# Respacing loads, in-place output blocks and weight differences in a fused attention and expert kernel

One core of one Trainium2 chip runs the kernel. The metric is the device time of one execution in microseconds, as the median of several. A run is called slow below when it is over 1.5% above the fastest of the same kernel; with one core there is no second die to compare with, so slow is only a matter of the time.

## The reference, cut

```python
def _attn_ref(x, state):            # x 8x8x512x64, state 8x8x32x64
    a = softmax(x @ state^T / 8);   xread = a @ state
    a2 = softmax(state @ x^T / 8);  sread = a2 @ x
    return concatenate([xread, sread], axis=2)      # 544 rows per batch and head

def _moe_ref(x, w_in, w_out, s, b): # x 4352x512, w_in 512x2048, w_out 2048x512
    r = maximum(x @ w_in, 0)
    return (s * (r * r) + b) @ w_out
```

The softmax lines are shortened; the reference subtracts the maximum and adds 1e-9 to the sum. All is given and returned in fp32.

## The kernel before

The kernel works on the eight batches as eight stages of 21 us. In a stage TensorE multiplies the hidden layer of one batch (`h`), the output of the batch before it (`oA`, `oB`, `oC`) and the scores of the next (`T`). The output product saves one multiplication in eight: it uses sums and differences of squares (`s`, formed by `token_sum`) and of weights (`wd`, formed by `weight_sums`), and drains banks A, B and C of PSUM (the memory that TensorE writes its sums into) several times. The parts that the change touches, with cuts marked by `# ...`:

```python
# the end of a block of the hidden layer: relu, then a square on VectorE or ScalarE
if key == 1 and f in (5, 9):
    with tc.issue_after(nc.cur_bb.bb.instructions[-1]):
        nc.scalar.square(gt[:, f % 4 - 1 : f % 4 + 1], r16)
elif f % 2 == 1:
    nc.vector.tensor_mul(gt[:, f % 4 - 1 : f % 4 + 1], r16, r16)
    G["last"] = nc.cur_bb.bb.instructions[-1]

# an output block: drain a bank of PSUM into a staging buffer (3 of them), then store it
def put(bank, add, j, n0):
    # ...
    osb = opool.tile([P, ni, NH], FP32, name=f"osb_{b}_{j}_{n0}", tag="osb")
    # ...
    nc.vector.scalar_tensor_tensor(osb, acc[bank], s_bc, add, ALU.mult, ALU.add)
    # ...
    nc.gpsimd.dma_start(dst[j][:, :, n0 : n0 + NH], osb)
# "add" is the bias for A, and the kept blocks u3, qb, u2 (one buffer each) for C, B, C
```

```python
# the opening
nc.scalar.dma_start(ident16, ident_dr.ap())
# ... two loads of half of batch 0's x, 512 KB each, on SyncE's queue
nc.scalar.dma_start(stf[:, 0:2, :], st_v[:, 0:2, :])
# ...
warm_up(11)                         # matmuls without use, 128x512
# ... casts of x
att_xT_pe(0, 0)                     # x transposed on TensorE, with ident16
att_stT(0)                          # state transposed on TensorE, with ident16
# ...
warm_up(2)
att_T(0, [0])                       # first scores

# stage s: f counts 16 steps of the hidden layer; at(f, ...) puts work behind step f
if s == 1:
    at(8, lambda: att_xT_dma(3))    # x of batch 3 transposed by DMA, SyncE's queue
    at(12, lambda: load_x(4))       # x of batch 4, 512 KB, GpSimd's queue
    # ...
if s == 2:
    at(1, lambda: load_x(5))
elif s in (3, 4):
    at(1, lambda: load_x(s + 3))
# ...
at(4, lambda: att_ET(nb))           # exponentials of the next batch transposed by DMA
at(8, lambda: att_shares(nb))       # VectorE: den (sums of ET), shares
if s in (2, 3):
    at(6, lambda: att_xT_dma(nb + 1))
at(9, lambda: att_a4_dma(nb))       # shares transposed by DMA
if s == 2:
    at(9, stT_dma)
elif s in (3, 4):
    at(9, lambda: att_xT_dma(s + 3))
```

The softmax here doesn't subtract the row's maximum and nothing guards it: scores larger than these inputs give would overflow.

Of the kernel before, what the change touches and what calls it, by code (L numbers as in the profile page):

```python
# [14 lines left out]
def kernel(  # L15
# [10 lines left out]
    nc = tc.nc  # L26
# [69 lines left out]
    stf = konst.tile([P, 2 * NPE, D], FP32, name="stf")  # L96
# [21 lines left out]
    def load_x(b):  # L118
        new_xn(b)
        nc.gpsimd.dma_start(  # L120
            out=xn[b].rearrange("p h c d -> p h (c d)"),
            in_=x[b].rearrange("h (q c) d -> q h (c d)", q=P),
        )
# [18 lines left out]
    A = {b: {} for b in range(B)}  # L142
# [59 lines left out]
    def att_xT_dma(b):  # L202
        xT = new_xT(b)
        nc.sync.dma_start_transpose(
            out=xT.rearrange("p h k t -> p (h k) t"),
            in_=xn[b].rearrange("p h c d -> p (h c d)"),
        )
# [180 lines left out]
    def mm1_close(key, hps, ntok, f):  # L388
        if f % 2 == 0:
            R2[key] = rpool.tile([P, 2, ntok], FP16, name=f"r_{key}_{f}", tag="r")  # L390
        r16 = R2[key]
        if key == 0 and f in (1, 5):
            nc.vector.tensor_scalar(r16[:, f % 2], hps, 0.0, None, ALU.max)
        else:
            nc.scalar.activation(r16[:, f % 2], hps, AF.Relu)  # L395
            G["relu"] = nc.cur_bb.bb.instructions[-1]
        if f % 4 == 0:
            G4[key, f // 4] = gpool.tile([P, 4, ntok], FP16, name=f"g_{key}_{f}", tag="g")
        gt = G4[key, f // 4]
        G[key, f] = gt[:, f % 4]  # L400
        if key == 1 and f in (5, 9):
            with tc.issue_after(nc.cur_bb.bb.instructions[-1]):
                nc.scalar.square(gt[:, f % 4 - 1 : f % 4 + 1], r16)
        elif f % 2 == 1:
            nc.vector.tensor_mul(gt[:, f % 4 - 1 : f % 4 + 1], r16, r16)  # L405
            G["last"] = nc.cur_bb.bb.instructions[-1]
# [111 lines left out]
    def fast_items(b):  # L518
# [41 lines left out]
        def put(bank, add, j, n0):  # L560
            if b == "sr":
                ends.append(own[1][:, len(ends) : len(ends) + 1])
                osb = ends[-1]
            else:
                osb = opool.tile([P, ni, NH], FP32, name=f"osb_{b}_{j}_{n0}", tag="osb")
            if bank == "C" and b == last_b:
                for i in range(ni):
                    nc.vector.scalar_tensor_tensor(
                        osb[:, i], acc["C", i], s_bc, add[:, i], ALU.mult, ALU.add
                    )  # L570
            else:
                nc.vector.scalar_tensor_tensor(osb, acc[bank], s_bc, add, ALU.mult, ALU.add)  # L572
            if b == "sr":
                for i in range(4):
                    dst = out_BSn[4 * j + i, S:ST, n0 : n0 + NH]
                    eng = nc.sync if i % 2 else nc.scalar
                    eng.dma_start(dst, osb[Ns * i : Ns * i + Ns, 0])
                return
            if b == "0b":
                nc.gpsimd.dma_start(x_dst(0, 2 + j)[:, n0 : n0 + NH], osb[:, 0])  # L580
                return
            dst = out_BSn[b, 0:S].rearrange("(q ci cj) n -> cj q ci n", ci=2, cj=2)
            nc.gpsimd.dma_start(dst[j][:, :, n0 : n0 + NH], osb)  # L583
# [74 lines left out]
    def bias_sum():  # L658
        ps = att_ps([P, DM], FP32, "wsum_ps")
        wsum = apool.tile([P, 2, DM], FP16, name="wsum", tag="W", bufs=1)  # L660
        for i in range(NKF // 4):
            for q in range(4):
                mm(
                    ps[32 * q : 32 * q + 32, :],
                    ones16,
                    wof(4 * i + q),
                    start=(i == 0),
                    stop=(i == NKF // 4 - 1),
                    tp=(0, 32 * q),
                )  # L670
        nc.vector.tensor_copy(wsum[:, 0], ps)
        nc.vector.tensor_sub(wsum[:, 1], ps, wsum[:, 0])
        A["wsum"] = wsum

    def bias_end():
# [18 lines left out]
    def warm_up(n):  # L694
        wps = psO.tile([P, 512], FP32, tag="o", name="warm_ps")
        for _ in range(n):
            mm(wps, warm[:, 0:P], warm)
# [12 lines left out]

    with tc.manual_schedule(engines={ET.PE, ET.SP, ET.Pool}):
        nc.vector.memset(warm, 0.0)
        nc.scalar.dma_start(ident16, ident_dr.ap())
        for g in range(NG):
            nc.sync.dma_start(
                xf[:, g],
                x[0, g :: NG].rearrange("h (q c) d -> q h (c d)", q=P),
            )
        nc.scalar.dma_start(stf[:, 0:2, :], st_v[:, 0:2, :])
        nc.scalar.preload_act_table_set("natural_log_exp_and_others")  # L720
        nc.sync.dma_start(stf[:, 2:4, :], st_v[:, 2:4, :])
        nc.sync.dma_start(sb_row[:, 0:1], moe_s.to_broadcast((1, 1)))
# [31 lines left out]
        nc.gpsimd.dma_start(out=st16[:, 4:, 0, :], in_=st_v[:, 4:, :])  # L754
        load_x(2)

        warm_up(11)
        cast_x0(0, 0, nc.vector.tensor_copy)
        cast_x0(0, 1, nc.scalar.copy)
        att_xT_pe(0, 0)  # L760
        att_stT(0)
        cast_x0(1, 0, nc.vector.tensor_copy)
        warm_up(2)
        att_T(0, [0])
# [37 lines left out]
        def pieces(s):  # L802
            nb = s + 1
            out = {}

            def at(f, fn):
                out.setdefault(f, []).append(fn)

            def ahead(f, fn):
                out.setdefault((f, "ahead"), []).append(fn)  # L810

            if s == 1:
                at(0, lambda: att_xT_dma(2))
                at(0, gated_x3)
                at(0, lambda: att_ET(0))
                at(0, lambda: att_ET(1))
                at(8, lambda: att_xT_dma(3))
                at(12, lambda: load_x(4))
                at(2, lambda: att_M(1, 2, "act"))
                ahead(3, bias_sum)  # L820
                at(4, bias_end)
                at(3, lambda: att_M(1, 3, "act"))
                at(6, lambda: att_stT(2))
                at(10, bias_half)
                at(8, lambda: att_M(2, 0, "act"))
                at(8, lambda: att_M(2, 1, "act"))
                at(10, lambda: att_M(2, 2, "act"))
                at(10, lambda: att_T(2, [0, 1]))
                at(11, lambda: att_ET(2))
                at(12, lambda: att_D(2, [0, 1]))  # L830
                at(13, lambda: att_M(2, 3, "act"))
                at(13, lambda: att_V(0))
                return out
            if s == 2:
                at(1, lambda: load_x(5))
            elif s in (3, 4):
                at(1, lambda: load_x(s + 3))
            if nb < B:
                if nb < NST:
                    at(0, lambda: att_stT(nb))  # L840
                ahead(4, lambda: att_M(nb, 0, "later"))
                ahead(4, lambda: att_T(nb, [0, 1]))
                ahead(4, lambda: att_M(nb, 1, "later"))
                at(4, lambda: att_ET(nb))
                at(4, lambda: A[nb]["M", 0]())
                at(6, lambda: A[nb]["M", 1]())
                at(8, lambda: att_shares(nb))
                if s in (2, 3):
                    at(6, lambda: att_xT_dma(nb + 1))
                at(9, lambda: att_a4_dma(nb))  # L850
                if s == 2:
                    at(9, stT_dma)
                elif s in (3, 4):
                    at(9, lambda: att_xT_dma(s + 3))
            if s == 2:
                at(1, lambda: att_srT_dma(0))
                at(8, lambda: att_V(1))
                at(12, lambda: att_srT_dma(1))
            ahead(4 if s == last_b else 10, lambda: att_V(s))
            if nb < B:  # L860
                ahead(10, lambda: att_M(nb, 2, "later"))
                ahead(10, lambda: att_M(nb, 3, "later"))
                at(10, lambda: A[nb]["M", 2]())
                at(12, lambda: A[nb]["M", 3]())
            if s == last_b:
                at(6, lambda: att_srT(s))
            else:
                at(12, lambda: att_srT_dma(s))
            if s == last_b:
                for i in range(4):  # L870
                    at(12 + i, lambda i=i: mm1_sr(i))
            return out
# [4 lines left out]
        for s in range(1, B):  # L877
# [16 lines left out]
            for f in range(NKF):  # L894
# [23 lines left out]
                    fn()  # L918
                if s == 1:
                    with tc.issue_after(G["last"]):  # L920
                        for _ in range({0: 2, 1: 1, 2: 1, 6: 1, 7: 1, 8: 1, 9: 1}.get(f, 0)):
                            sums.pop(0)()
                        for i, j in {0: [(1, 0), (2, 0)], 1: [(1, 1), (2, 1)], 7: [(3, 0)], 8: [(3, 1)],
                                     10: [(4, 0), (4, 1)]}.get(f, []):
                            token_sum("0b", i, j)
                for fn in items[f]:
# [57 lines left out]
```

## Time and profile before

| | before |
|---|---|
| time, median of 3 (range) | 209.41 us (209.28 to 209.71) |
| span of the profiled run | 208.0 us |
| TensorE busy | 198.5 us (95%) |
| end of its last matmul | 203.73 us |

The waits and lines at the four gaps of TensorE that the change aims at stand in the prediction below. Five more lines, of the timeline of before, are needed for what came. The columns are the start in us, the duration in us, engine (a "q" means a DMA being issued), line, operation, output and inputs; in brackets stands the idle time in front of it with what ended it.

```profile
7.36 0.59 PE L70 MATMUL warm_ps<-warm 128*128 128x512 f16 x2
...
96.05 1.01 POOL L120 DMA_DIRECT2D xn<-in_x_dram  x1
...
103.59 2.17 SPq L330 DMA_TRANSPOSE ET<-E  x1
...
109.22 1.22 DVE L278 TENSOR_REDUCE den<-ET 128x32 f32<-128x1024 f16 x1
...
111.83 0.60 PE L70 MATMUL oC<-wo,s 128*128 128x256 f16 x4
```

The load of batch 7's x leaves 7.5 us ahead of the transpose ET. ET is issued at 103.59, landed at 108.60 by its semaphore (5.0 us), `den` reads it without a wait, and behind `den` VectorE drains bank C in time for the oC at 111.83, which waits for nothing. In the first line two warm-up matmuls take 0.59 us together and start 0.22 us apart; the eleven at the start came every 0.43 us. So TensorE's array, the grid that multiplies, ran at half its rate at first and at full rate by 7.36.

### The profile page before, as it was taken

How to read it: one execution, taken by the hardware profiler on the slowest of the kernel's cores; microseconds unless marked ns; L12 is line 12 of the kernel's file. 1: busy time of each engine (PE TensorE's matmuls, PEld its weight loads, DVE VectorE, ACT ScalarE, POOL GpSimd, SP SyncE). 2: the span in 40 equal slices, each digit the busy share in tenths (PEclk: the TensorE clock that was granted, in tenths of full speed). 3: DMA queues.
4: the chain of work that ended last, by engine and by line, in shares of the span. 5: the costliest groups of instructions: out<-in, count | busy, mean ns of one | idle time of the engine just before them, and what ended most of it. 6: DMA issues, size and time to landing. Idle time of an engine off the chain costs nothing.

```text
span 208.0 us, 4853 instructions
## 1 busy us (share of the span) xinstructions
PE 198.5 (95%) x1971; PEld 133.0 (64%) x1971; DVE 163.4 (79%) x286; ACT 128.5 (62%) x254; POOL 39.3 (19%) x66
## 2 busy tenths in 40 slices
PE   7988999998999999999999999999999999999991
PEld 2433333555766676667676667676767777788881
DVE  1479688987859996799779966997699786796861
ACT  2478966799577666767676658675957555543100
POOL 5690002413210230023002101120112012100210
PEclk9999999999999999999999999999999999999999
DMA  6999996997999397929961944160416011200243
GB/s 185 221 201 206 207 191 97 183 181 172 139 182 194 98 184 90 191 80 197 150 104 53 139 121 104 50 158 3 101 38 158 19 50 50 98 7 0 74 141 94
DMA packets 46795, 25.55 MB, mean 123 GB/s; under 512 B 31732, under 2 KB 44788, under 8 KB 46772
## 3 DMA queue, kind: packets, MB, share of 16 engines
q0 software_dynamic: 15568, 16.19, 39.8%
q1 hardware_dynamic: 30180, 8.49, 24.3%
q10 hardware_dynamic: 1024, 0.56, 1.0%
q8 instruction: 15, 0.25, 0.5%
q14 instruction: 8, 0.07, 0.2%
HBM read 17.33 MB, written 8.91 MB: 126 GB/s over the span
## 4 chain that ended last, share of the span: by engine, by line
PE 84%; DMA 5%; DVE 4%; ACT 3%; issue 1%; POOL 1%; ACTq 0%
PE h L70 24%; PE oB L70 18%; PE oC L70 11%; PE oA L70 11%; PE Mps L70 4%; PE o L70 3%; PE h_sr L70 3%; DMA stf<-in_state_dram 3%; DMA a<-aT 2%; ACT r L395 2%; PE V L70 1%; PE oB_sr L70 1%; PE T L70 1%; PE oB_0b L70 1%; PE oC_0b L70 1%
## 5 line engine op out<-in xcount | busy, mean ns | idle before, releaser
L395 ACT ACTIVATE r<-h 128x512 f16<-128x512 f32 x126 | 74.3, 602 | 45.0 <-PE h L70 45.0
L70 PE MATMUL h<-a,M 128*128 128x512 f16 x256 | 74.2, 379 | 1.4 <-DVE M L320 0.6
L70 PEld LDWEIGHTS <-s 128*128 128x128 f16 x448 | 43.7, 98 | 15.8
L405 DVE TENSOR_TENSOR g<-r 128x1024 f16<-128x1024 f16 x62 | 42.2, 683 | 12.8 <-ACT r L395 12.1
L70 PEld LDWEIGHTS <-g 128*128 128x128 f16 x392 | 37.2, 98 | 18.5 <-issue 4.4
L583 POOL DMA_DIRECT2D out_dram<-osb x27 | 18.3, 676 | 124.2 <-DVE osb L572 51.6
L70 PE MATMUL oB<-wd,s 128*128 128x256 f16 x224 | 32.8, 272 | 0.0
L70 PE MATMUL oA<-wo,g 128*128 128x256 f16 x224 | 32.5, 273 | 0.0
L70 PEld LDWEIGHTS <-M 128*128 128x128 f16 x256 | 24.3, 98 | 12.3 <-issue 2.1
L297 ACT CAST M<-Mps 128x1024 f16<-128x1024 f32 x20 | 20.1, 1007 | 0.0
L70 PE MATMUL oC<-wd,s 128*128 128x256 f16 x112 | 16.5, 273 | 0.0
L70 PE MATMUL oB<-wd,g 128*128 128x256 f16 x112 | 15.7, 273 | 0.0
L70 PE MATMUL oC<-wo,s 128*128 128x256 f16 x112 | 15.3, 273 | 0.0
L608 DVE SCALAR_TENSOR_TENSOR u<-oB,s_bc,qa 128x512 f32<-128x512 f32 x7 | 5.2, 749 | 7.6 <-PE oB L70 7.6
L395 ACT ACTIVATE r_sr<-h_sr 128x256 f16<-128x256 f32 x16 | 6.1, 383 | 7.9 <-PE h_sr L70 7.3
L234 ACT ACTIVATE E<-T 128x256 f16<-128x256 f32 x20 | 7.4, 385 | 4.0 <-PE T L70 4.0
L514 DVE TENSOR_TENSOR s<-s,g 128x1024 f16<-128x1024 f16 x14 | 9.6, 686 | 0.2
L70 PE MATMUL h_sr<-srdT,wi 128*128 128x256 f16 x64 | 9.6, 273 | 0.0
L516 DVE TENSOR_TENSOR s<-g,s 128x1024 f16<-128x1024 f16 x14 | 9.6, 685 | 0.0
L507 DVE TENSOR_TENSOR s<-g 128x1024 f16<-128x1024 f16 x14 | 9.6, 684 | 0.0
L512 DVE TENSOR_TENSOR s<-g,g 128x1024 f16<-128x1024 f16 x14 | 9.6, 683 | 0.0
L572 DVE SCALAR_TENSOR_TENSOR osb<-oC,s_bc,u 128x512 f32<-128x512 f32 x12 | 8.9, 745 | 0.4 <-PE oC L70 0.4
(126 smaller groups left out, 226.5 us busy)
## 6 DMA issues: line engine op xcount, KB each, us to landing
out_dram<-osb POOLq DMA_DIRECT2D x29, 256.0 KB, 2.8
xn<-in_x_dram POOLq DMA_DIRECT2D x7, 512.0 KB, 8.8
wi<-in_moe_w_in_dram POOLq DMA_DIRECT2D x4, 512.0 KB, 8.4
wo<-in_moe_w_out_dram POOLq DMA_DIRECT2D x4, 512.0 KB, 15.1
xf<-in_x_dram SPq DMA_DIRECT2D x2, 512.0 KB, 4.8
out_dram<-osb_0b POOLq DMA_DIRECT2D x4, 128.0 KB, 6.2
out_dram<-osb_sr SPq DMA_DIRECT2D x8, 32.0 KB, 1.6
out_dram<-osb_sr ACTq DMA_DIRECT2D x8, 32.0 KB, 1.7
```

The costliest lines, as they stand in the source:

```text
L70: return nc.tensor.matmul(out, lhsT, rhs, start=start, stop=stop, tile_position=tp, is_transpose=is_transpose, skip_group_check=True,)
L234: nc.scalar.activation(a["E"][:, g, 256 * m : 256 * m + 256], Ts[m][:, g, :], AF.Exp, scale=scale, accum_out=a["rs"][:, NG * m + g : NG * ...
L297: nc.scalar.copy(dst, ps)
L395: nc.scalar.activation(r16[:, f % 2], hps, AF.Relu)
L405: nc.vector.tensor_mul(gt[:, f % 4 - 1 : f % 4 + 1], r16, r16)
L507: nc.vector.tensor_sub(o, a11, a21)
L512: nc.vector.tensor_add(o, a21, a22)
L514: nc.vector.tensor_sub(o, SQ[b, 1, j], a11)
L516: nc.vector.tensor_sub(o, a12, SQ[b, 2, j])
L572: nc.vector.scalar_tensor_tensor(osb, acc[bank], s_bc, add, ALU.mult, ALU.add)
L583: nc.gpsimd.dma_start(dst[j][:, :, n0 : n0 + NH], osb)
L608: nc.vector.scalar_tensor_tensor(u, acc["B"], s_bc, kept["qa"], ALU.mult, ALU.add)
```

## The change

Its intent, as its parts read: have the state rows early so that the state is transposed before x; spare VectorE's output blocks the staging buffers; spread the differences of weights so that bank B is drained sooner; and pull loads of x apart from transposes.

```diff
--- before.py
+++ after.py
@@ -398,7 +398,7 @@
             G4[key, f // 4] = gpool.tile([P, 4, ntok], FP16, name=f"g_{key}_{f}", tag="g")
         gt = G4[key, f // 4]
         G[key, f] = gt[:, f % 4]
-        if key == 1 and f in (5, 9):
+        if key == 1 and f in (3, 5):
             with tc.issue_after(nc.cur_bb.bb.instructions[-1]):
                 nc.scalar.square(gt[:, f % 4 - 1 : f % 4 + 1], r16)
         elif f % 2 == 1:
@@ -561,6 +561,8 @@
             if b == "sr":
                 ends.append(own[1][:, len(ends) : len(ends) + 1])
                 osb = ends[-1]
+            elif bank != "A":
+                osb = add
             else:
                 osb = opool.tile([P, ni, NH], FP32, name=f"osb_{b}_{j}_{n0}", tag="osb")
             if bank == "C" and b == last_b:
@@ -670,6 +672,7 @@
                 )
         nc.vector.tensor_copy(wsum[:, 0], ps)
         nc.vector.tensor_sub(wsum[:, 1], ps, wsum[:, 0])
+        G["last"] = nc.cur_bb.bb.instructions[-1]
         A["wsum"] = wsum
 
     def bias_end():
@@ -710,13 +713,13 @@
 
     with tc.manual_schedule(engines={ET.PE, ET.SP, ET.Pool}):
         nc.vector.memset(warm, 0.0)
+        nc.scalar.dma_start(stf[:, 0:2, :], st_v[:, 0:2, :])
         nc.scalar.dma_start(ident16, ident_dr.ap())
         for g in range(NG):
             nc.sync.dma_start(
                 xf[:, g],
                 x[0, g :: NG].rearrange("h (q c) d -> q h (c d)", q=P),
             )
-        nc.scalar.dma_start(stf[:, 0:2, :], st_v[:, 0:2, :])
         nc.scalar.preload_act_table_set("natural_log_exp_and_others")
         nc.sync.dma_start(stf[:, 2:4, :], st_v[:, 2:4, :])
         nc.sync.dma_start(sb_row[:, 0:1], moe_s.to_broadcast((1, 1)))
@@ -754,11 +757,12 @@
         nc.gpsimd.dma_start(out=st16[:, 4:, 0, :], in_=st_v[:, 4:, :])
         load_x(2)
 
-        warm_up(11)
+        warm_up(9)
+        att_stT(0)
+        warm_up(2)
         cast_x0(0, 0, nc.vector.tensor_copy)
         cast_x0(0, 1, nc.scalar.copy)
         att_xT_pe(0, 0)
-        att_stT(0)
         cast_x0(1, 0, nc.vector.tensor_copy)
         warm_up(2)
         att_T(0, [0])
@@ -834,7 +838,7 @@
             if s == 2:
                 at(1, lambda: load_x(5))
             elif s in (3, 4):
-                at(1, lambda: load_x(s + 3))
+                at(8, lambda: load_x(s + 3))
             if nb < B:
                 if nb < NST:
                     at(0, lambda: att_stT(nb))
@@ -845,13 +849,13 @@
                 at(4, lambda: A[nb]["M", 0]())
                 at(6, lambda: A[nb]["M", 1]())
                 at(8, lambda: att_shares(nb))
-                if s in (2, 3):
+                if s == 2:
                     at(6, lambda: att_xT_dma(nb + 1))
                 at(9, lambda: att_a4_dma(nb))
                 if s == 2:
                     at(9, stT_dma)
-                elif s in (3, 4):
-                    at(9, lambda: att_xT_dma(s + 3))
+                elif s in (3, 4, 5):
+                    at(9, lambda: att_xT_dma(s + 2))
             if s == 2:
                 at(1, lambda: att_srT_dma(0))
                 at(8, lambda: att_V(1))
@@ -918,9 +922,9 @@
                     fn()
                 if s == 1:
                     with tc.issue_after(G["last"]):
-                        for _ in range({0: 2, 1: 1, 2: 1, 6: 1, 7: 1, 8: 1, 9: 1}.get(f, 0)):
+                        for _ in range({0: 2, 1: 1, 2: 1, 3: 1, 6: 1, 9: 2}.get(f, 0)):
                             sums.pop(0)()
-                        for i, j in {0: [(1, 0), (2, 0)], 1: [(1, 1), (2, 1)], 7: [(3, 0)], 8: [(3, 1)],
+                        for i, j in {0: [(1, 0), (2, 0)], 1: [(1, 1), (2, 1)], 3: [(3, 0)], 7: [(3, 1)],
                                      10: [(4, 0), (4, 1)]}.get(f, []):
                             token_sum("0b", i, j)
                 for fn in items[f]:
```

## The prediction

> **What bounds the kernel now.** I read the page first, then the waits of TensorE alone, then the timeline around each of its gaps, then the list of DMA issues around the tiles that those gaps name, and last the order in which the built programs stand, engine by engine.
>
> ```profile
> PE 198.5 (95%) x1971; PEld 133.0 (64%) x1971; DVE 163.4 (79%) x286; ACT 128.5 (62%) x254; POOL 39.3 (19%) x66
> ...
> PE h L70 <- DVE M L320: 0.6, 1, 0.6
> PE oC_0b L70 <- DVE osb_0b L572: 0.5, 1, 0.5
> PE h L70 <- DMA a<-aT: 0.5, 1, 0.5
> PE oB_0b L70 <- DVE u_0b L608: 0.5, 1, 0.5
> PE T L70 <- ACT xT L197: 0.4, 1, 0.4
> PE warm_ps L70 <- DVE M L320: 0.4, 1, 0.4
> PE stTps L70 <- POOL st L734: 0.3, 1, 0.3
> ...
> 204.00:208.00 4.00, 0.00 (x0) 0.00 (x0) 0.25 (x1) 0.00 (x0) 0.00 (x0) 1.00 0.29 82
> ```
>
> TensorE is busy for 198.5 us of 208.0 at full clock. Of the other 9.5, 1.2 lie before its first matmul and 4.2 after its last, where only output is drained; the change touches neither. So all that can be won without fewer matmuls is about 4 us of gaps, and the change has as many matmuls as before. It aims at four of these gaps (stTps, oB_0b, oC_0b, h behind the a transpose): 0.32 + 0.48 + 0.54 + 0.49 = **1.83 us, 0.9%**, is the ceiling, apart from what a shorter opening brings. The question is which of the four goes, and what comes in its place.
>
> [...] identity and state rows left ScalarE's queue 0.43 us apart and landed 3.7 us apart. [...] here a 256 KB store takes 2.5 us when alone and 5 to 8 us in traffic. [...] forming a block in place should cost VectorE nothing, and 128x512 takes 0.75 us either way (osb 745 ns, u 749 ns).
>
> **1. State rows ahead of the identity.**
>
> ```profile
> 0.74 0.39 ACTq L713 DMA_DIRECT2D ident<-ident_const  x1
> 1.17 0.59 ACTq L719 DMA_DIRECT2D stf<-in_state_dram  x1
> ...
> 5.86 1.06 PE L70 MATMUL xTps<-ident,xn 128*128 128x128 f16 x8
> 6.79 0.40 POOL L734 CAST st<-stf 128x256 f16<-128x256 f32 x1 [3.13 <-DMA stf<-in_state_dram]
> 7.24 0.29 PE L70 MATMUL stTps<-ident,st 128*128 128x128 f16 x2 [0.32 <-POOL st L734]
> 7.91 0.30 PE L70 MATMUL T<-xT,stT 64*32 64x256 f16 x8
> ```
>
> The first scores (T) start at 7.91, when the transposed state is copied; the transposed x would let them start at 7.54. The state came late because its rows, second on the queue, landed at 6.73; the identity, first, at 3.03. After the change TensorE does nine warm-up matmuls (1.19 + 9 x 0.427 = 5.03), then the state transposes, two more warm-ups, then the x transposes. If both loads are there by 5.0, x transposes start at 5.03 + 0.12 + 0.85 = 6.0. VectorE's new order puts a cast that waits for the second half of x (landed 6.79) ahead of its copy of the transposed x, which then ends at 6.8 + 0.42 + 0.42 = 7.64: T at 7.7, **0.2 us won**. But the identity is now second, where 64 KB waited until 6.7, and both transposes need it. If it lands at about 6.1, TensorE stands 1.0 us at the state transposes, and T starts near 8.9: **1.0 us lost**. I give these 0.5 and 0.3, and 0.2 to no difference: +0.2 us on average.
>
> **2. Weight differences and squares around batch 0's second half.** TensorE's own order is unchanged there. In VectorE's order two of the eight weight differences and a 512-wide one go earlier, the last two later, behind the square of blocks 8 and 9, which moves from ScalarE to VectorE while that of 2 and 3 goes the other way.
>
> ```profile
> 42.67 0.48 DVE L608 SCALAR_TENSOR_TENSOR u_0b<-oB_0b,s_bc,qa_0b 128x256 f32<-128x256 f32 x1
> 42.86 0.63 ACT L395 ACTIVATE r<-h 128x512 f16<-128x512 f32 x1
> 43.20 0.60 PE L70 MATMUL oB_0b<-wd,s_0b 128*128 128x256 f16 x4 [0.48 <-DVE u_0b L608]
> 45.37 0.48 DVE L613 SCALAR_TENSOR_TENSOR u_0b<-oB_0b,s_bc,qa_0b 128x256 f32<-128x256 f32 x1
> 48.37 0.48 DVE L572 SCALAR_TENSOR_TENSOR osb_0b<-oC_0b,s_bc,u_0b 128x256 f32<-128x256 f32 x1 [1.04 <-PE oB_0b L70]
> 48.91 0.27 PE L70 MATMUL oC_0b<-wo,s_0b 128*128 128x256 f16 x1 [0.54 <-DVE osb_0b L572]
> ```
>
> Bank B is drained twice (the two u_0b), and each time TensorE must wait before it adds to the bank. The first drain moves up from 42.67 to about 41.4, when its products are done: **0.48 won**. The second stands behind more work now. The square of 8 and 9 can't start before ScalarE's r at 42.86 + 0.63 = 43.5; then come four 128x1024 operations at 0.60 from start to start (square, two differences, one s) and two of 0.36: 43.5 + 2.4 + 0.7 = 46.6. The drain ends at 47.1. TensorE reaches its next matmul into bank B at 46.47 - 0.48 = 46.0, and waits: **about 1.17 lost**, as a wait of oB_0b for u_0b again, but at the other line.
>
> **3. Three of four blocks in place.** The osb_0b wait ends, by the view, with PE oB_0b. That product is no input of it; its own was done at 46.6. It writes a staging buffer whose earlier store was issued at 40.2 and took 8.1 us, so landed at 48.2: this is the wait, and the in-place block does not have it. VectorE can drain C by about 48.7, before TensorE, now some 0.7 late, is back: **0.54 won**.
>
> In place has its own price: u2, u3 and qb have one buffer each, and the next batch's write must wait until the store of the last has landed. A batch lasts 21.1 us. For u3 and qb there are over 10 us of slack. u2 is drained last and needed first:
>
> ```profile
> out_dram<-osb_0b POOLq DMA_DIRECT2D x1, 128.0 KB, 7.1
> ...
> 58.27 0.75 DVE L608 SCALAR_TENSOR_TENSOR u<-oB,s_bc,qa 128x512 f32<-128x512 f32 x1 [1.35 <-PE oB L70]
> 59.83 0.49 PE L70 MATMUL oB<-wd,s 128*128 128x256 f16 x3
> ```
>
> The last store of batch 0 left at 52.94 behind a 512 KB load of x and landed at 60.1. The u of batch 1, at 58.27, would have to wait for it: 60.1 + 0.75 = 60.9, against 59.83 + 0.15 where TensorE wants bank B. **About 0.95 lost**, at 0.8 likely since it hangs on one landing. At the later batches the store takes 5.3 to 5.5 us at worst and lands at about the moment when u is drained (100.8 against 100.93), and TensorE has 0.8 us of slack more: nothing.
>
> **4. Loads and transposes of x.** No wait of TensorE names xT or xn. The 0.49 at 118 comes from an a transpose that took 5.0 us, issued at 113.09 with the xT transpose behind it at 114.54. That pair stays; one like it now also stands at batch 6. I count 0, give or take 0.5.
>
> **Sum.** +0.2 - 0.48 + 1.17 - 0.54 + 0.8 x 0.95 + 0 = **+1.1 us**, or 210.5.
>
> **Rivals.** *The intent holds*: the identity is early, the second drain and the store of u2 cost nothing, and the 0.49 goes too. Then 209.4 - 1.7 = 207.7. For it: positions so particular look like the outcome of trials. Against it: the order of VectorE and the single buffer are in the built program, and only their times can differ. *The identity is late and all new waits come*: +1.0 + 0.15 + 0.95 + 0.5 = 212.0. *A shift of load*: ScalarE, 7.5 of 7.6 us busy from 42.7 to 50.3, loses a square of 1 us there; if that brings all its relus forward, part of the 1.17 may not come, and the time is about 209.5. VectorE does not become a bound: 79% before, and it gets no work.
>
> **Range and chances.** The sum says 210.5, the intent 207.7. Since the positions look tried, I move part of the way: 209.9, with 207.9 to 211.4 for eight in ten. 2% is 4.2 us, more than all gaps aimed at, and twice what I see lost: faster 0.01, same 0.96, slower 0.03.
>
> **What would show it.** TensorE's waits should no longer name osb_0b; they should name u_0b once, for 1.0 to 1.2 us near 47, and u near 60 for up to 1 us, with VectorE idle before that u for over 2 us. At the opening, T before 7.8 or after 8.7 decides part 1; a wait of stTps for the identity's DMA shows the loss. The a wait near 118 should stay within 0.5 us. I am wrong if u_0b is drained by 46, if the last store of batch 0 lands before 58.5, or if a stage in the middle, 21.1 us before, changes its length.

## More of the kernel before

DMAs issued by GpSimd share one queue: q0 of before's page moved 16.19 MB, the sum of GpSimd's 49 issues, and all 49 landed in the order of the program. So did the 21 of SyncE's 27 transposes whose landing before's trace holds.

## The result and the profile after

| | before | after |
|---|---|---|
| median of six runs | 209.34 us | 212.38 us |
| range | 209.19 to 209.71 | 210.81 to 214.87 |
| ratio of the fast runs (95% interval) | | 1.011 (1.0067 to 1.0153) |
| end of the last matmul, profiled run | 203.73 us | 208.79 us |

A ratio is the mean time of one kernel's fast runs over that of the other's in the same rounds, so it isn't quite the ratio of the two medians. The change lies within 2%, but on the slow side, and beyond the range predicted. Two things changed, not one: the time went up, and its spread from run to run went from 0.5 to 4 us. (Part of that contrast is luck: in the four groups of later runs, before itself spread over 2.6 to 2.7 us in 11 runs.) The profiled run of after is its longest, 214.87. So its trace shows what can happen in this kernel, and what happens in the fast runs has to come from other profiles.

The first line of busy times and the waits of TensorE, after:

```profile
PE 200.8 (94%) x1971; PEld 134.0 (63%) x1971; DVE 163.7 (77%) x286; ACT 128.6 (60%) x254; POOL 38.7 (18%) x66
...
PE oC L70 <- DVE u L574: 2.1, 1, 2.1
PE stTps L70 <- DMA ident<-ident_const: 1.4, 1, 1.4
...
PE oB_0b L70 <- DVE u_0b L615: 1.1, 1, 1.1
```

There are as many matmuls as before, but TensorE is busy for 2.3 us longer: it ran part of them slower. Of the waits that the change aimed at, osb_0b, the first u_0b and the a transpose are gone. In their place stand three others. The timeline shows each.

**The opening, after:**

```profile
1.29 0.53 ACTq L717 DMA_DIRECT2D ident<-ident_const  x1
...
6.66 0.37 PE L70 MATMUL stTps<-ident,st 128*128 128x128 f16 x2 [1.45 <-DMA ident<-ident_const]
6.82 1.06 PE L70 MATMUL warm_ps<-warm 128*128 128x512 f16 x2
...
9.52 0.41 PE L70 MATMUL T<-xT,stT 64*32 64x256 f16 x8
```

The identity, now second on ScalarE's queue behind a state load, landed at 6.62 (before: 3.03), and TensorE stood 1.45 us. Then the pair of warm-up matmuls took 1.06 us where before's pair at 7.36 took 0.59: the array was still at half its rate (0.43 us from start to start), and stayed there until about 10.5 (transposes start 0.11 us apart up to 10.48, and 0.06 us apart at 11.92). The first scores moved from 7.91 to 9.52.

**The second drain of bank B:**

```profile
48.33 0.48 DVE L615 SCALAR_TENSOR_TENSOR u_0b<-oB_0b,s_bc,qa_0b 128x256 f32<-128x256 f32 x1
48.86 0.38 PE L70 MATMUL oB_0b<-wd,g 128*128 128x256 f16 x2 [1.15 <-DVE u_0b L615]
```

This is the wait that part 2 of the prediction worked out, at the other line and with the size predicted.

**Near 114:**

```profile
105.28 2.80 SPq L330 DMA_TRANSPOSE ET<-E  x1
...
106.40 0.90 POOL L120 DMA_DIRECT2D xn<-in_x_dram  x1 [0.19 <-PE h L70]
...
113.89 1.22 DVE L278 TENSOR_REDUCE den<-ET 128x32 f32<-128x1024 f16 x1 [2.90 <-DMA ET<-E]
115.03 0.74 DVE L574 SCALAR_TENSOR_TENSOR u<-oC,s_bc,u 128x512 f32<-128x512 f32 x1
...
115.83 0.60 PE L70 MATMUL oC<-wo,s 128*128 128x256 f16 x4 [2.15 <-DVE u L574]
```

Against the five lines of before: the load of x now leaves 1.1 us behind ET in place of 7.5 us ahead of it. ET landed at 113.87, after 8.59 us. VectorE stood 2.90 us at `den`, until 113.89; the drain of bank C, behind it in VectorE's program, started at 115.03; TensorE stood 2.15 us. And a window of the table by stretches (us, busy time of each engine, then the granted clock of TensorE) shows what followed:

```profile
116.34:119.75 3.41, 3.41 (x13) 1.64 (x12) 3.41 (x6) 0.73 (x2) 1.36 (x2) 0.50 0.50 129
```

The granted clock is at 0.50 for 3.41 us. Seven matmuls oC took 1.70 us there, and 0.93 us in before.

**Where the 5.06 us of the profiled run went**, from the gaps in the two traces:

| place | before | after | difference |
|---|---|---|---|
| opening, up to the h that waits for M | 18.00 | 19.73 | +1.73 |
| first u_0b, osb_0b, a near 118 | 0.48 + 0.54 + 0.49 | no longer | -1.51 |
| second u_0b | none | 1.15 | +1.15 |
| oC near 114 | none | 2.15 | +2.15 |
| half clock behind it: 3.41 us for what takes half | none | 1.71 | +1.71 |
| sum | | | +5.23 |

0.17 us too much; where it goes I did not follow. Without the two rows near 114 the sum is 1.37 us. The fast runs are on average 2.3 us (1.1% of 209.4) above before, so in some of them more than those 1.37 must be lost too.

### The profile page after: what moved, and what is told of

It is laid out like the page before. It is cut to its first block, busy times and chain, and to the rows that moved or that the text cites. A ratio compares the mean times of both kernels' runs of the same rounds, so it can differ in the third digit from the quotient of the medians.

```text
span 213.1 us, 4851 instructions
## 1 busy us (share of the span) xinstructions
PE 200.8 (94%) x1971; PEld 134.0 (63%) x1971; DVE 163.7 (77%) x286; ACT 128.6 (60%) x254; POOL 38.7 (18%) x66
## 4 chain that ended last, share of the span: by engine, by line
PE 82%; DMA 7%; DVE 5%; ACT 4%; issue 1%; ACTq 0%
PE h L70 23%; PE oB L70 16%; PE oA L70 11%; PE oC L70 11%; DMA ET<-E 4%; PE o L70 3%; PE Mps L70 3%; PE h_sr L70 3%; DMA ident<-ident_const 3%; ACT r L395 2%; PE warm_ps L70 1%; PE oB_sr L70 1%; PE V L70 1%; PE T L70 1%; DVE g L405 1%; DVE M L320 1%
## 5 line engine op out<-in xcount | busy, mean ns | idle before, releaser
L70 PE MATMUL h<-a,M 128*128 128x512 f16 x256 | 75.2, 384 | 0.9 <-DVE M L320 0.6
L405 DVE TENSOR_TENSOR g<-r 128x1024 f16<-128x1024 f16 x62 | 42.7, 691 | 12.5 <-ACT r L395 11.9
L585 POOL DMA_DIRECT2D out_dram<-u x13 | 8.8, 676 | 55.7 <-DVE inv L280 26.1
L70 PE MATMUL oC<-wo,s 128*128 128x256 f16 x112 | 16.1, 282 | 2.1 <-DVE u L574 2.1
L70 PE MATMUL oB<-wd,g 128*128 128x256 f16 x112 | 15.7, 273 | 0.0
L585 POOL DMA_DIRECT2D out_dram<-osb x7 | 4.7, 677 | 59.0 <-DVE rt L335 29.9
L574 DVE SCALAR_TENSOR_TENSOR u<-oC,s_bc,u 128x512 f32<-128x512 f32 x12 | 8.9, 745 | 1.0 <-PE oC L70 1.0
```

What stands on the lines that cost most here:

```text
L70: return nc.tensor.matmul(out, lhsT, rhs, start=start, stop=stop, tile_position=tp, is_transpose=is_transpose, skip_group_check=True,)
```

## Experiments

**Theory.** The loss has three parts: the late identity, the second drain of bank B, and a load of x that the respacing put beside the transpose ET. The third is also taken to be why the time varies. **Rivals.** The in-place blocks make the waits, through their single buffers. Or it is not the load of x that delays ET but the transposes of x that moved with it. All kernels gave correct results. Five rounds each, beside runs of before on the same chip (median 209.26 to 209.71, range 208.14 to 211.29 over the four groups of runs).

### Undo one part

`e1_undo_load`: only the loads go back.

```diff
-                at(8, lambda: load_x(s + 3))
+                at(1, lambda: load_x(s + 3))
```

> The changed kernel with one part undone: the loads of x for batches 6 and 7 stand at block 1 of their stage again, not at block 8. Theory: the load of batch 7, issued in the same microsecond as the ET transpose of batch 5, makes that transpose take 8.6 us in place of 5.0; VectorE waits for it in order and TensorE loses 2.1 us near 114 and then runs 3.4 us at half clock. Then this run has no TensorE wait for u near 114, no half clock, ET back at about 5 us, and 2 to 3 us less than the changed kernel: about 210.7 us, with little spread between runs. Rival (the buffers used in place, or the moved xT transposes, cause the wait near 114): it stays, the time stays at 211 to 215 with the same spread.

Measured: median 215.70 (211.74 to 219.75), ratio 1.017 (1.011 to 1.024). It got worse, so the simple form of the theory failed. ET took 6.66 us here and nothing waits for it, but the load, issued at 97.82, now stands 2.7 us behind a transpose of x issued at 95.10, as it did in before. But the change had also put another batch in that place: before, it was the x of batch 6, needed a stage later; now it is that of batch 5, needed at 103.4. TensorE waits for it:

```profile
105.83 0.44 PE L70 MATMUL T<-xT,stT_all 64*32 64x256 f16 x16 [2.39 <-DMA xT<-xn]
```

Loads and transposes can only be judged together. The run has one more wait that after's profile lacks: at 61.68 `oB` stood 1.14 us for a `u` that waited for the last store of batch 0 (see e2). It also tells of the opening. The identity landed at the same time as in after, TensorE stood as long (1.49 us), and yet:

```profile
6.81 0.59 PE L70 MATMUL warm_ps<-warm 128*128 128x512 f16 x2
...
8.21 0.60 PE L70 MATMUL T<-xT,stT 64*32 64x256 f16 x8
```

Here the array was already at its full rate (0.59 us for the pair), the scores started at 8.21 and not 9.52, and the h that waits for M stood at 18.59, +0.59 against before. So the wait for the identity costs 0.6 us in this run; the other 1.1 us in after's profile come from the array at half rate. The wait may be what brings it: of the seven profiles that wait for the identity (1.0 to 2.1 us), four ran at half rate somewhere between 6.4 and 10.9 us (after, e3, e4, e5) and three did not (e1, e8, e13), and none of the other eleven, with gaps of up to 1.4 us near 7, was at half rate after 7.3. Why it comes in some runs only is not shown.

`e2_undo_open`: only the opening goes back (identity first, 11 warm-ups, state transposed behind x).

```diff
-        nc.scalar.dma_start(stf[:, 0:2, :], st_v[:, 0:2, :])
         nc.scalar.dma_start(ident16, ident_dr.ap())
...
+        nc.scalar.dma_start(stf[:, 0:2, :], st_v[:, 0:2, :])
-        warm_up(9); att_stT(0); warm_up(2)
+        warm_up(11)    # and att_stT(0) behind att_xT_pe(0, 0)
```

> The changed kernel with the opening undone: identity ahead of the state rows, x transposes ahead of the state transposes. Theory: the identity, second on its queue, landed at 6.66 us and TensorE stood 1.45 us for it; without that the first T starts at 7.9 and not at 9.5, and all 1.6 us of that reach the end: ratio to before about 1.003 in a run that does not have the wait near 114. Rival (the loads that follow set the pace, so the opening is hidden): T starts at 7.9 but the last stages end where they ended, less than 0.5 us won.

Measured: 212.48 (210.56 to 217.65), ratio 1.010 (1.005 to 1.016). The scores are back at 7.93, but the time is not. With the early opening everything reaches batch 1 some 1.7 us sooner, and there the wait for the single buffer stands, which after does not show:

```profile
61.48 0.75 DVE L610 SCALAR_TENSOR_TENSOR u<-oB,s_bc,qa 128x512 f32<-128x512 f32 x1 [4.57 <-DMA out_dram<-u_0b]
62.29 0.80 PE L70 MATMUL oB<-wd,s 128*128 128x256 f16 x3 [2.31 <-DVE u L610]
```

That is the price of in-place blocks from part 3 of the prediction. The last store of batch 0 landed at 61.39. In after it landed at 59.85, and u came at 59.96: the late opening hid this wait. A half clock came with it, from 62.18 to 65.59, in this run, which is a slow one (214.09, mean granted clock 0.992).

`e3_undo_sq`: only the squares and weight differences go back.

```diff
-        if key == 1 and f in (3, 5):
+        if key == 1 and f in (5, 9):
-        G["last"] = nc.cur_bb.bb.instructions[-1]        # in bias_sum
-     for _ in range({0: 2, 1: 1, 2: 1, 3: 1, 6: 1, 9: 2}.get(f, 0)):
+     for _ in range({0: 2, 1: 1, 2: 1, 6: 1, 7: 1, 8: 1, 9: 1}.get(f, 0)):
-     ... 3: [(3, 0)], 7: [(3, 1)],
+     ... 7: [(3, 0)], 8: [(3, 1)],
```

> The changed kernel with the places of the two ScalarE squares and of the weight differences undone. Theory: the 1.15 us wait of oB_0b for the second u_0b near 48 goes, the 0.48 us wait for the first one comes back, the osb_0b wait stays away: 0.65 us less than the changed kernel. Rival (VectorE is full there either way): a wait of the same length at another place, no change.

Measured: 212.53 (212.12 to 213.35), ratio 1.015 (1.012 to 1.019). The first wait of oB_0b for u_0b is back at 0.48 us and the second is gone, as part 2 of the prediction has it. That should have been worth 0.67 us and the median did not move. Its profiled run, 213.35 and fast, has the wait near 114 again (ET 8.54 us, TensorE 2.10 us), and a granted clock of 0.50 in the opening from 7.30 to 10.71. So the wait near 114 is not a thing of slow runs alone.

`e4_undo_inplace`: only the in-place blocks go back to staging buffers.

```diff
-            elif bank != "A":
-                osb = add
```

> The changed kernel with all blocks in staging buffers again. Theory: the in-place form costs nothing here; the osb wait near 49 returns only in so far as the store that it waits for (landed at 48.9 in the changed kernel) lands after VectorE gets there, at 49.7, so it does not return: no change within 0.3 us. The wait of u for the store of u near 145 (1.7 us) goes, worth nothing on TensorE. Rival (in place is what makes stores and transposes late): the wait near 114 goes and 2 us are won.

Measured: 212.37 (210.97 to 214.41), ratio 1.014 (1.009 to 1.019). Nothing gained, and the spread stayed, so the rival of the single buffers falls as the sole cause of it. The osb_0b wait did not come back either: the earlier store landed at 48.02, and bank C was drained only at 49.47, for the second u_0b wait had made it later. In the changed kernel as a whole, in-place blocks win nothing. The profiled run (210.97, fast) has the load of x at the same place, 1.1 us behind ET, and ET took 4.88 us: no wait near 114.

### Both loads and transposes, or one part alone

`e5_undo_load_xT` puts loads and transposes of x back and leaves the rest; `e6_only_load_xT` has only them.

```diff
# e6, against before (e5 the other way, against after)
-                at(1, lambda: load_x(s + 3))
+                at(8, lambda: load_x(s + 3))
-                if s in (2, 3):
+                if s == 2:
                     at(6, lambda: att_xT_dma(nb + 1))
-                elif s in (3, 4):
-                    at(9, lambda: att_xT_dma(s + 3))
+                elif s in (3, 4, 5):
+                    at(9, lambda: att_xT_dma(s + 2))
```

> The changed kernel with both the loads and the transposes of x at their old places. The first undoing showed that the loads alone are not it: with the old loads the xT transpose of batch 5, now one batch later than before, waited among them and TensorE lost 2.4 us at T near 103. Theory: each late transpose of x has lost a stage of slack, and any traffic beside it or beside the ET transpose reaches TensorE; with both undone no wait above 1 us is left after 64 us, and the spread falls from 4 us to that of the kernel before (under 1.5 us); what remains is the opening (+1.6), the second u_0b (+1.15), less 0.48 and 0.54: about 211 us, unless the u near 60 waits for a store. Rival (the in-place buffers make the spread): it stays at 4 us.

Measured: 211.14 (210.29 to 213.97), ratio 1.006 (1.002 to 1.010). In its profile (fast) no wait over 0.5 us stands behind 64 us; what is left is the opening (T at 9.15, again at half rate: 1.06 us for the warm-up pair at 6.45) and the second u_0b. The spread did not fall below 1.5 us as expected: five runs lie within 1.3 us, but the sixth is at 213.97.

> The kernel before with the loads and transposes of x respaced and nothing else. Theory: this part brings the spread and a wait of about 2 us at one of two places (T for xT, or oC for a drained block behind the ET transpose near 110) in part of the runs: 209.4 to 213, median near 210.5. Rival: it is harmless without the other parts: 209.4 within 0.3 and no wait above 0.6 us.

Measured: 210.87 (209.22 to 213.64), ratio 1.004 (0.999 to 1.008). Its profiled run, a slow one, shows the wait with none of the other parts there:

```profile
112.60 1.22 DVE L278 TENSOR_REDUCE den<-ET 128x32 f32<-128x1024 f16 x1 [2.94 <-DMA ET<-E]
...
114.53 0.60 PE L70 MATMUL oC<-wo,s 128*128 128x256 f16 x4 [2.19 <-DVE osb L572]
```

The five profiled kernels with the load 1.1 us behind ET had ET landing after 8.59 (after), 5.94 (e2), 8.54 (e3), 4.88 (e4) and 8.63 us (e6). In the twelve other profiles in which the load left 7 to 10 us ahead of this ET (before and e1 among them) it took 4.6 to 6.7 us. So it took over 8 us in three of five profiles with the load beside it and in none without. e1 and e13 (below) keep the moved transposes and only move the load, and had 6.66 and 4.26 us; the rival that the moved transposes delay ET falls. At 8.5 us and more the transpose came later than VectorE had use for it: VectorE stood 2.90 us at `den` in after and 2.94 us in e6.

`e7_only_inplace` has only the in-place blocks, `e8_only_open` only the opening, each against before.

```diff
# e7
+            elif bank != "A":
+                osb = add
# e8
+        nc.scalar.dma_start(stf[:, 0:2, :], st_v[:, 0:2, :])
         nc.scalar.dma_start(ident16, ident_dr.ap())
...
-        nc.scalar.dma_start(stf[:, 0:2, :], st_v[:, 0:2, :])
-        warm_up(11)    # and att_stT(0) behind att_xT_pe(0, 0)
+        warm_up(9); att_stT(0); warm_up(2)
```

> The kernel before with three of four blocks in place and nothing else. Theory: the osb_0b wait (0.54) goes, and the u of batch 1 near 58 waits for the last store of batch 0 to land at about 60 to 61: TensorE loses 1.0 to 2.3 us at oB. In the changed kernel the late opening hid this wait (u came at 59.96, the store landed at 59.85). So 209.9 to 211.2, slower than before. Rival (the store lands earlier when nothing else is changed): 208.9.

Measured: 211.51 (209.56 to 214.66), ratio 1.005 (0.999 to 1.012). The osb_0b wait is gone, and VectorE stands 3.03 us at the u of batch 1 for the store of u_0b (issued 52.59, landed 59.09); TensorE did not wait at oB, where 1.0 to 2.3 us were expected. The runs above 212 were not explained by this profile, which is of the fastest run. But it has a first hint of their cause: T waits 0.8 us, until 58.95, for a transpose of x that took 10.3 us, with a load of x issued 0.24 us ahead of it.

> The kernel before with the new opening and nothing else. Theory: the identity lands at about 6.6, T starts at 9.5 in place of 7.9, and the 1.6 us stay to the end: 211.0. Rival (later waits for transfers that are paced by themselves swallow it, as the u wait did in the changed kernel): under 0.6 us.

Measured: 210.61 (209.84 to 211.03), ratio 1.004 (1.000 to 1.008). The identity landed at 6.18 and TensorE stood 1.0 us. The array was at full rate from 6.3 (0.59 us for the warm-up pair), T came at 7.73, and the end of TensorE's work stayed at 203.73. The part costs little in this profile, which is of the fastest run, and wins nothing; the median is 0.9 us above that of before beside it.

### Mend each part

`e9_inplace_but_u2`: in place, except for the block that is needed first by the next batch.

```diff
+            elif bank != "A" and not (b == "0b" and add is kept["u2"]):
+                osb = add
```

> The kernel before with blocks in place, except that the last block of batch 0 goes through a staging buffer again, so that the u of batch 1 has no store to wait for. Theory: the runs at 212.5 to 214.7 of the in-place kernel came from that store (TensorE about 2 us at oB near 60, then 3.4 us at half clock); they go, the osb_0b wait (0.54) is gone too: 208.9 to 209.4, spread as before. Rival (the tail comes from the in-place u3 and qb, or from load C issued earlier): runs above 212 stay.

Measured: 209.04 (208.36 to 211.62), ratio 0.998 (0.994 to 1.001). No wait for osb_0b, none for u; TensorE ends at 202.26. No run is above 212, but one is slow at 211.62, so the spread is not quite that of before's fast runs.

`e10_ident_on_sp`: the opening, with the identity first on SyncE's queue and the state rows first on ScalarE's.

```diff
+        nc.scalar.dma_start(stf[:, 0:2, :], st_v[:, 0:2, :])
+        nc.sync.dma_start(ident16, ident_dr.ap())
-        nc.scalar.dma_start(ident16, ident_dr.ap())
```

> The kernel before with the new opening, but the identity leaves SyncE's queue ahead of x while the state rows stay first on ScalarE's. Theory (a small load behind another one on its queue comes after the large loads): both small loads are first on their queues, the identity lands at about 3.1, the state rows at about 4.8 as in the changed kernel, TensorE does not wait for the identity; the x rows land up to 0.4 later. T between 7.6 and 8.1: 0.2 won to 0.2 lost. Rival (the identity needs 6 us whenever it stands beside the state rows): it lands after 5.5, T after 8.7.

Measured: 209.35 (208.51 to 210.24), ratio 1.000 (0.996 to 1.004). Both small loads, each first on its queue, are there early (identity 2.65 against 6.62 in after, state 2.86 against 6.73 in before, where they were second), TensorE has no gap, and T starts at 6.96, 0.95 us sooner than before and sooner than the 7.6 to 8.1 expected. The gain is eaten at once: the next product waits 0.71 us for the first weights, until 10.52, which landed no sooner (in before it started at 10.41).

`e11_sq_inplace_mended` takes e9 and part 2 with the last weight differences put directly behind the first u_0b; `e12_mended_and_ident` adds the opening of e10.

```diff
# e11, against the change
+                if b == "0b":
+                    G["u2"] = nc.cur_bb.bb.instructions[-1]      # p == 6, the first drain of bank B
-                    with tc.issue_after(G["last"]):
+                    with tc.issue_after(G["u2"] if f == 9 else G["last"]):
```

> The kernel before with the parts that should pay, mended: squares and weight differences moved as in the change, but the last two differences directly behind the first drain of u_0b in place of behind the square of blocks 8 and 9; blocks in place but for the last of batch 0; opening, loads and transposes of x as before. Theory: no wait at oB_0b and none at oC_0b, so 0.48 + 0.54 us less than before: ratio 0.995, TensorE's last matmul near 202.7. Rival (VectorE is too full there and the second drain is late all the same): oB_0b waits 0.5 to 1.1 for the second u_0b, no gain.

> The same with the opening of the run before it but one (identity on SyncE's queue). Theory: the sum of the two, 0.9 to 1.2 us less than the kernel before, ratio 0.9945 to 0.9955. Rival: the moves of one part hide those of the other, as the late opening hid the u wait in the changed kernel: then the sum is off by over 0.5 us.

Measured: e11 210.16 (208.20 to 217.53), ratio 1.000; e12 209.64 (208.37 to 217.19), ratio 1.000. Both waits at u_0b are gone or down to 0.2 us, and the best run of e11 is the best so far, but two runs of six and two of seven are far longer. The expected gain did not come. The profile of e12 fell on a long one (217.19):

```profile
47.19 0.91 POOL L120 DMA_DIRECT2D xn<-in_x_dram  x1
...
48.57 6.92 SPq L204 DMA_TRANSPOSE xT<-xn  x1
...
64.29 0.65 PE L70 MATMUL T<-xT,stT 64*32 64x256 f16 x16 [6.82 <-DMA xT<-xn]
```

It is the same pattern at another place. Once the staging wait is gone, GpSimd's queue gets to its next entry sooner, and that is the load of x for batch 4. It now leaves ahead of the transpose of batch 3's x, which took 15.7 us and which T needs at 57.5. In before that load left at 49.68, 1.9 us behind the transpose. That the load is the cause was open still; so was whether the load alone makes the wait near 114.

### Move one load

`e13_after_load_at_12`: the changed kernel, its two loads four steps later, away from ET.

```diff
-                at(8, lambda: load_x(s + 3))
+                at(12, lambda: load_x(s + 3))
```

> The changed kernel in full, except that the loads of x for batches 6 and 7 leave at f 12 of their stage in place of f 8, so that they are no longer issued within 1.2 us of the exponentials' transpose (ET) and the store of block A. Theory (load beside ET causes the wait near 114 and, through it, the half clock and the spread): ET near 105 lands within 6 us of its issue in place of 8.59, no TensorE wait over 1 us between 108 and 116, no run over 212.5, median 210.5 to 211.3, ratio to before 1.005 to 1.009 (the late opening and the second u_0b wait stay). Rival (the transposes of x or the earlier parts cause it): ET still takes over 8 us, the wait of about 2 us stays, the median stays near 212 with runs over 213.

Measured: 220.68 (220.02 to 227.47), ratio 1.053 (1.049 to 1.058). Half of the expectation came: ET lands after 4.26 us, and no wait of TensorE for u stands near 114. The total is far off, and a reason is plain in the trace (the profiled run is the long one):

```profile
98.37 4.77 SPq L204 DMA_TRANSPOSE xT<-xn  x1
98.49 1.02 POOL L120 DMA_DIRECT2D xn<-in_x_dram  x1
...
111.17 0.65 PE L70 MATMUL T<-xT,stT_all 64*32 64x256 f16 x16 [4.46 <-DMA xT<-xn]
```

Moved away from one transpose the load stands 0.1 us behind the next, and now T waits 4.46 us, with another 2.08 us in the next stage. So the load went with a late transpose at both of its places: ET after 8.59 us in after, and here an x transpose for which T waited 4.46 us. All six runs besides the profiled one are above 220, so this is no matter of luck any more. Not all of the 227 is the load's: the profile also has the wait of oB for u near 63 (3.48 us, the store of e2), another of 1.47 us near 139, and 13.65 us of half clock in all (mean granted clock 0.965).

`e14_inplace_load4_later`, `e15_mended_load4_later`, `e16_mended_ident_load4_later`: e9, e11 and e12, each with the load for batch 4 behind the last store of batch 0.

```diff
-                at(12, lambda: load_x(4))
+                at(14, lambda: load_x(4))
```

> In-place blocks alone (u2 of batch 0 still staged), as the earlier run with the same blocks, and the load of x for batch 4 two places later, behind the last store of batch 0 in GpSimd's queue. Theory (that load ahead of the x transpose of batch 3 is what can delay it): this kernel had the transpose ahead of the load already in its profile, so little changes in the profile: median 208.5 to 209.3, but no run over 210.5 of five. Rival (the tail has another cause): a run over 211 among them again.

> The mended weight differences and in-place blocks, and the load of x for batch 4 behind the last store of batch 0. Theory: the x transpose of batch 3 (issued near 49, landed 58.9 in the same kernel with the load ahead of it) lands before 56.5, T does not wait for xT near 58, no run over 211, median 208.0 to 208.8, ratio .992 to .997. Rival (the transpose is late because of the two stores, or because it is itself issued later): it lands after 58 again, T waits for xT again, runs over 212 among five.

> The same as the run before, with the identity on SyncE's queue as well. Theory: as that run, within 0.3 us of it either way (the identity was shown to bring nothing by itself); xT of batch 3 lands before 56.5 where 64.2 was seen with the load ahead. Rival: again runs over 215.

| | load ahead or between: median (range) | load behind: median (range), ratio |
|---|---|---|
| in place but u2 (e9, e14) | 209.04 (208.36 to 211.62) | 208.82 (208.45 to 209.73), 0.996 (0.992 to 1.000) |
| with weight differences (e11, e15) | 210.16 (208.20 to 217.53) | 208.70 (208.13 to 208.97), 0.995 (0.991 to 0.999) |
| with the opening too (e12, e16) | 209.64 (208.37 to 217.19) | 208.11 (207.66 to 209.26), 0.993 (0.989 to 0.997) |

With the load left where it was, 5 of 19 runs were slow; with it behind, none of 18. The expectations of e14 and e15 came; e16 lies 0.6 us below e15 where 0.3 at most was expected, but their intervals overlap. The two columns come from different chips, but each has before beside it, whose own medians were 209.26 and 209.71. In e16:

```profile
47.10 2.99 SPq L204 DMA_TRANSPOSE xT<-xn  x1
...
52.24 1.81 POOL L120 DMA_DIRECT2D xn<-in_x_dram  x2
```

The transpose lands at 52.51, after 5.4 us where it took 15.7 us in e12, and T starts at 57.29 without a wait. This kernel is better than both of those compared, by 0.7% against before; that is below 2%, yet its interval does not reach 1.

## Why the prediction was wrong, step by step

**The failed step is part 4**, "I count 0, give or take 0.5". The prediction looked at which transposes stand near each other and never at where the moved load comes to stand. That load, 1.1 us behind ET, makes ET take 8.5 to 8.6 us in some runs, and then costs 2.15 us and 1.7 us of half clock: +3.9 us in after's profile. The prediction's own sign of being wrong came with it: the stage around 114, 21.1 us in before, lasted 25.1. e6 shows it with this part alone, and e1 and e13 show that the load carries it (ET 6.66 and 4.26 us with the load elsewhere). The profiles of after and e6 are of slow runs, where it costs most. Over the fast runs the part costs some 0.8 to 1.1 us, by an estimate from the ratios: 1.004 (0.999 to 1.008) alone in e6, and 1.011 with it against 1.006 without it in e5. The wait for a that part 4 thought would stay went, for 0.49 us. The sentence "No wait of TensorE names xT or xn" misreads its own list, where T waits 0.4 us for xT; that one is a copy of an x transposed on TensorE, and nothing hangs on it. Its "5 to 8 us in traffic" for a 256 KB store is too narrow as well: in before's trace they took 2.5 to 2.6 us alone and up to 8.1 us, several of them 3 to 5 us.

**Part 1: the loss was named, but its chance and its size were off.** "If it lands at about 6.1, TensorE stands 1.0 us at the state transposes, and T starts near 8.9" had a chance of 0.3; it landed late in each of the seven profiles with this opening (6.2 to 6.7). The queue order was the right reason, as e10 shows: first on SyncE's queue the identity landed at 2.65. That sum counts a warm-up at half rate, 0.43 us, and for a landing at 6.6 in place of 6.1 it would give 9.4; after has 9.52. What it has no term for is that the array's rate differs from run to run (after the wait for the identity a warm-up pair took 1.06 us in after and e5, 0.59 us in e1, e3 and e8). At the h that waits for M the opening costs 0.1 to 0.6 us where the array was at full rate behind the gap (e8, e13, e1), and 1.3 to 1.7 us where it was not, or fell back (e3, e5, e4, after).

**Part 2 held**, in mechanism and size: -0.48 at the first drain, and 1.15 us against 1.17 worked out at the second. The drain ended at 48.81 in place of 47.1; that is the prediction's time plus the 1.7 us by which all was late. So the rival of a shift of load, by which part of the 1.17 would not come, fell.

**Part 3 held in its first half**: no wait for osb_0b. But e4 shows that in this kernel it would have gone without in-place blocks too. The wait for u, 0.95 us at 0.8, did not come in after, where the late opening gave the store the time it needed; in e2 without that opening it was 2.31 us, and in e1, whose opening cost only 0.6 us, it was 1.14 us. The mechanism was right, and the prediction treated as independent two parts that are not.

**The sum** was +1.1 us before the pull towards the intent, and the fast runs give +2.3 us. For the difference of 1.2 us the estimate for part 4 and the opening (1.004 alone in e8, about 0.8 us where +0.2 was expected) are about enough, with intervals as wide as the difference itself. The pull to 209.9 was a further error: "the positions look tried" carried 0.6 us of weight, and no trace supported it. The range failed at its upper end since it had no term for a wait that comes in some runs only. Why a given fast run is at 210.8 and another at 213.0 stays open: only one execution of each kernel has a trace.

**The rivals.** "The intent holds" fell. "The identity is late and all new waits come", 212.0, is near in time but for the wrong reason: it has no load beside ET in it, and its u wait did not come in after's profile.

## What to carry to other kernels

Before a large load is moved, list every transfer that lies within some microseconds of its new place, and ask which of them an engine needs soon: here a 512 KB load of x made TensorE wait 2.2, 4.5 or 6.8 us, by which transpose it stood beside (after, e13, e12), and not at all once it stood behind the last store of a batch (e16). Taking away a wait on an engine that issues DMAs can move the transfers behind it in its queue (the load of x for batch 4 left at 47.19 in e12 and at 49.68 in before), so look at the new order of that queue and not only at the gap that closed. And where the time of a changed kernel scatters more than that of the old one, look for a wait whose length differs from run to run before averaging it away.

## What these runs show of transfers and of the clock

- The DMA transpose of the exponentials near 105 took 4.3 to 6.7 us with no load issued beside it, and 4.9 to 8.6 us with a 512 KB load issued 1.1 us behind; a transpose of x took 5.4 us with the load behind a store (e16), and 15.7 us with the load 1.4 us ahead (e12).
- Two small loads on one queue: beside two 512 KB loads of x on SyncE's queue, the first of them issued in the same moment, the identity (32 KB) landed 2.1 to 2.3 us after its issue when first on ScalarE's queue and after 4.9 to 5.4 us when second; the state rows (64 KB) after 4.0 to 4.6 us when first and 5.0 to 5.7 us when second. With the identity ahead of the loads of x on SyncE's queue (e10, e12, e16) the state rows took 2.1 to 2.2 us and the identity 1.9 to 2.0 us.
- A half clock followed some gaps of TensorE and not others. It came with a gap of 2.15 us in after (113.68 to 115.83), for 3.41 us; with one of 2.31 us in e2, for 3.41 us from just before the end of the gap; and with one of 2.19 us in e6, where the granted clock was 0.60 on average from 115.0 to 118.5. It also followed gaps of 1.94 us and 2.08 us in the openings of e3 and e4, for 3.42 us each. A gap of 2.39 us in e1 and of 2.10 us near 113 in e3 had none, so the length of the gap alone does not decide; what else does is not shown here.
- The array was at half rate at the start of these runs, and the moment of change differs from run to run: matmuls from 1.19 on, full rate from about 4.0 us in e3 (an estimate from its nine warm-up matmuls, which took 3.43 us in place of 4.02) and from between 6.6 and 7.3 us in before, and with a gap of 1.45 us in the warm-up only near 10.5 us in after. The windows view prints a granted clock of 1.00 for all of this stretch of after; only the spacing of equal matmuls (0.43 against 0.22 us) shows it.
